# Bits of the keys as signs on ScalarE, the first head taken apart by VectorE alone, an expert picked by integer bits

## The chip, the cores and the metric

The kernel runs on one core of a Trainium2 chip. Its engines run side by side and wait for each other by semaphores: TensorE (PE in the rows; PEld is its weight load), VectorE (DVE), ScalarE (ACT), GpSimd (POOL) and SyncE (SP), which issues most transfers. The metric is the device time of one execution in microseconds, the median of several runs.

## The reference

Two layers follow each other. The first is attention in which a query sees only the keys of its own bucket; a bucket is the signs of six projections.

```python
q_bits = (np.einsum('bhsd,dk->bhsk', q, proj) > 0).astype(np.int64)   # k_bits likewise
q_bucket = np.sum(q_bits * powers, axis=-1)
mask = q_bucket[:, :, :, None] == k_bucket[:, :, None, :]
scores = np.where(mask, scale * np.matmul(q, k.transpose(0, 1, 3, 2)), -1000000000.0)
attn = np.exp(scores - np.max(scores, axis=-1, keepdims=True))
attn = attn / (np.sum(attn, axis=-1, keepdims=True) + 1e-09)
return np.matmul(attn, v)
```

There are 4 batches, 8 heads, 768 positions and 64 numbers per head. The result, 3072 tokens of 512 numbers, goes through a mixture of 8 experts: each token to the one expert with the largest logit, `h = relu(x @ w1[e])`, `y = h @ w2[e]`, weighted by the expert's probability.

## The kernel before

**Attention.** Two heads make a group, and there are 16 groups. A score tile is 128 queries by 768 keys; a group has 12 of them, all together 192 units. A step `c` of the main loop makes two scores, so there are 96 steps, and the steps overlap: in step `c` TensorE multiplies the weights of step `c-5` by the values (`pv`, L346), transposes the exponentials of step `c-2` in three batches of four (`trans`, L314) and makes two scores (`score`, L278 and L280). VectorE takes each score's row maximum (L285) and makes its factors (L286, L287), ScalarE the exponential (L295). A score tile has two places in PSUM, so score `i` waits for exponential `i-2`. Three places (`t`) serve the transposes, the projections of a group and the token rows.

**Taking apart.** Each 32-bit input is split in a rounded part and a rest, and both multiply. `qk` (later `w`) of a head has four planes of 768 columns: plane 0 is q rounded over q's rest, plane 1 is k rounded, plane 2 and plane 3 hold 80 rows: 16 rows of bits and the rest of the parts. `score` multiplies planes 0 and 1 (L280) and planes 2 and 3 (L278). The bits are scaled by a large number M0, so that a pair of different buckets falls far below every other score.

**Bits.** For a later group, `lsh_mm` (L232) projects both heads, `lsh_ev` (L243) copies the projections from PSUM, `lsh_bits` turns them into bits by two GpSimd operations (q's half at L237, k's half at L239, through the helper `bits`), and a store and a gather put them in the planes. For the two heads of the first group `lsh_first` (L217) projects, and `bits_first` makes the bits by VectorE straight from PSUM: for halves 0 and 1 of q at L237, for the halves 2 and 3 of k at L239. `split_first` takes these two heads apart with VectorE, ScalarE and GpSimd.

**The opening.** The order on every engine is the order in which the code is written. After the constants come `lsh_first(0)`, `split_first(0, 0)`, bits, `lsh_first(1)`, `split_first(1, 0)`, one bit operation, and then the loop with unit 0. The first three units are of head 0, the next three of head 1. In between `warmth` issues matmuls of ones (L99) that nothing reads.

**The pick.** Near the end of attention VectorE works out which expert has most tokens so far, in three steps of a generator (`pick_first`): keys (`keys`, L454 to L457), their maximum (L464, L466), and the expert's number (L468 to L471); SyncE loads it and starts to fetch that expert's weights. The loop takes the steps at `c` = NC-13, NC-11 and NC-10, where NC is 96. In the same stretch `tok_ev` (L375) scales token rows out of a `t` place.

Of the kernel before, what the change touches and what calls it, by code (L numbers as in the profile page):

```python
# [7 lines left out]
F32 = mybir.dt.float32  # L8
# [4 lines left out]
OP = mybir.AluOpType  # L13
# [17 lines left out]
M0 = float(2 ** 35)  # L31
# [10 lines left out]
WARM = 10  # L42
# [8 lines left out]
def lsh_attention_moe(ctx, tc, qk, qk2, v, proj, wg, w1, w2, out):  # L51
# [35 lines left out]
    load_x(1)  # L87
    ones = const.tile([128, 128], BF16, name="ones")
# [27 lines left out]
    lt6, lt12, eq12, thr, mul = (const.tile([128, 1], F32, name=n) for n in ("lt6", "lt12", "eq12", "thr", "mul"))  # L116
# [3 lines left out]
    nc.vector.tensor_scalar(thr, lt6, -LOW, LOW, op0=OP.mult, op1=OP.add)  # L120
    nc.vector.tensor_scalar(lt6, lt6, 1.5 * M0, None, op0=OP.mult)
# [64 lines left out]
    def split_first(h, half):  # L186

        x = XD[h]
        c = slice(half * HALF, (half + 1) * HALF)
        if half == 0:  # L190
            t = qk_tile(h)
            for a in range(2):
                nc.scalar.activation(t[:, 1, a * HALF:(a + 1) * HALF], x[:, S + a * HALF:S + (a + 1) * HALF], AF.Copy)
        t = QK[h]

        def copy(o, i):
            if half:
                nc.gpsimd.tensor_copy(o, i)
            elif h:
                nc.scalar.activation(o, i, AF.Copy)  # L200
            else:
                nc.vector.tensor_copy(o, i)

        copy(t[:, 0, c], x[:, c])
        copy(t[0:80, 2, c], x[0:80, c])
        (nc.gpsimd if h or half else nc.vector).tensor_tensor(t[64:128, 0, c], x[64:128, c], t[64:128, 0, c],
                                                              op=OP.subtract)
        if half == 0:
            for a in range(2):
                nc.gpsimd.tensor_tensor(  # L210
                    t[0:80, 3, a * HALF:(a + 1) * HALF], x[0:80, S + a * HALF:S + (a + 1) * HALF],
                    t[0:80, 1, a * HALF:(a + 1) * HALF], op=OP.subtract)
# [7 lines left out]

    def bits_first(h, a):
        bits(QK[h][0:16, 2 + a // 2, (a % 2) * HALF:(a % 2 + 1) * HALF], LP[-h][32 * a:32 * a + 16, :HALF],
             a < 2, thr[0:16], mul[0:16])
# [11 lines left out]
    def bits(o, i, q, th, mu, eng=nc.vector):  # L235
        if q:
# [532 lines left out]
    for c in range(NC + 2):  # L769
# [28 lines left out]
        if c and c <= NC:  # L798
            expo(2 * c - 2)
        if lsh:  # L800
            lsh_ev(g + 1)
# [215 lines left out]
```

## Time and profile before

| what | us |
|---|---|
| median of 3 runs (lowest, highest) | 794.73 (794.68, 794.74) |
| the profiled execution | 794.61 |
| its span | 792.8 |
| PE busy | 779.3 (98%) |
| POOL busy | 508.9 (64%) |
| DVE busy | 467.6 (59%) |
| ACT busy | 443.8 (56%) |

The profile is of one execution. Busy time of an engine is the time in which it has an instruction under way; the ends of matmuls are modelled, so a wait of TensorE that is shorter than such a tail does not show as idle time, but as a longer distance of one matmul to the next. PEclk is the share of full speed that the clock throttle granted; whether a matmul ran at the full or at the half level shows in the distances as well.

### The profile page before, as it was taken

The numbers are of one execution on the slowest core, as the hardware profiler recorded it, in microseconds if no ns is written. First come the engines' busy times: TensorE is split into PE (matmuls) and PEld (weight loads), VectorE is DVE, ScalarE is ACT, GpSimd is POOL, SyncE is SP. The second block draws the span as 40 slices with busy tenths as digits, with TensorE's granted clock in tenths as the row PEclk, the third lists the DMA queues.
The fourth block names the chain that finished last, engine by engine and source line by source line (L and its number), as shares of the span: only waits on it lengthen the run. The fifth ranks groups of instructions, "written<-read, shape, count | busy, mean of one in ns | idle before, by whom it ended". The sixth has DMA issues, their size and how long they took to land.

```text
span 792.8 us, 13715 instructions
## 1 busy us (share of the span) xinstructions
PE 779.3 (98%) x4829; PEld 617.1 (78%) x4829; DVE 467.6 (59%) x1092; ACT 443.8 (56%) x877; POOL 508.9 (64%) x620
## 2 busy tenths in 40 slices
PE   8999999999999999999999999999999999999995
PEld 4677677776677777777777768989999999989894
DVE  7777777877777777777787855232363632232221
ACT  4776676776767766677676741443434344434310
POOL 7877475686747678746769473585566666668431
PEclk9999999999999999999999999999999999999999
DMA  8389953265234236313336214844445455545201
GB/s 300 121 223 274 297 165 102 75 190 165 101 100 160 94 112 205 100 62 119 110 109 182 80 54 142 279 161 156 159 151 162 145 148 178 165 146 195 85 10 36
DMA packets 48071, 115.31 MB, mean 145 GB/s; under 512 B 8820, under 2 KB 12660, under 8 KB 48001
## 3 DMA queue, kind: packets, MB, share of 16 engines
q1 hardware_dynamic: 41184, 98.05, 38.9%
q0 software_dynamic: 6672, 16.35, 6.7%
q8 instruction: 39, 0.64, 0.3%
q14 instruction: 32, 0.25, 0.1%
q10 hardware_dynamic: 144, 0.02, 0.0%
HBM read 88.39 MB, written 26.51 MB: 145 GB/s over the span
## 4 chain that ended last, share of the span: by engine, by line
PE 89%; DVE 4%; issue 4%; POOL 1%; ACT 1%; DMA 1%; POOLq 0%; DVEq 0%; ACTq 0%
PE o L346 17%; PE t L314 16%; PE t L675 15%; PE t L701 9%; PE s L278 8%; PE s L280 8%; PE s L718 7%; PE t L365 4%; DVE m L285 2%; PE t L232 1%; PE s L727 1%; PE t L651 1%; PE s L675 1%; PE o L651 1%; POOL w L617 1%
## 5 line engine op out<-in xcount | busy, mean ns | idle before, releaser
L295 ACT ACTIVATE e<-s,m 128x768 f32<-128x768 f32 x192 | 190.4, 992 | 126.2 <-DVE m L287 123.8
L285 DVE TENSOR_REDUCE m<-s 128x1 f32<-128x768 f32 x192 | 182.9, 953 | 67.0 <-PE s L280 58.0
L617 POOL TENSOR_TENSOR w<-raw,w 128x512 fp32r<-128x512 f32 x112 | 142.4, 1295 | 44.5 <-ACT w L616 43.0
L314 PEld LDWEIGHTS t<-ident,e 128*128 128x128 f32 x1152 | 125.5, 140 | 42.5 <-issue 19.8
L314 PE MATMUL t<-ident,e 128*128 128x128 f32 x1152 | 147.3, 277 | 1.0 <-ACT bits L243 0.8
L346 PE MATMUL o<-pt,vt 128*64 128x384 f32 x768 | 144.8, 499 | 0.0
L675 PE MATMUL t<-xh,w 128*128 128x456 f32 (+6 forms) x672 | 126.9, 346 | 0.0
L675 PEld LDWEIGHTS t<-xh,w 128*128 128x128 f32 x672 | 119.2, 188 | 3.0
L336 ACT ACTIVATE pt<-t 128x512 f32<-128x512 f32 (+1 forms) x194 | 104.1, 593 | 1.1 <-PE t L314 1.0
L346 PEld LDWEIGHTS o<-pt,vt 128*64 128x64 f32 x768 | 46.6, 136 | 58.1 <-issue 54.5
L680 DVE SCALAR_TENSOR_TENSOR hh<-t,hh 128x256 fp32r<-128x256 f32 (+7 forms) x64 | 35.5, 554 | 89.2 <-ACT hh L679 87.8
L701 PE MATMUL t<-hh,w 128*128 128x456 f32 (+3 forms) x384 | 78.6, 358 | 0.0
L679 ACT ACTIVATE hh<-t 128x256 fp32r<-128x256 f32 (+7 forms) x64 | 31.4, 491 | 78.0 <-PE t L675 76.7
L731 POOL DMA_INDIRECT out_dram<-y,ix x27 | 26.9, 995 | 73.4 <-DVE y L729 32.7
L334 DVE COPY pt<-t 128x512 f32<-128x512 f32 (+1 forms) x97 | 66.1, 683 | 12.4 <-PE t L314 12.2
L701 PEld LDWEIGHTS t<-hh,w 128*128 128x128 f32 x384 | 69.9, 188 | 2.3
L616 ACT ACTIVATE w<-raw 128x512 fp32r<-128x512 f32 x112 | 66.3, 623 | 0.0
L718 PE MATMUL s<-w,hh 128*128 128x512 f32 (+2 forms) x264 | 64.5, 398 | 0.0
L237 POOL TENSOR_SCALAR bits<-bits 64x384 f32<-64x384 f32 x15 | 22.6, 1509 | 54.6 <-ACT bits L243 54.6
L718 PEld LDWEIGHTS s<-w,hh 128*128 128x128 f32 (+2 forms) x264 | 47.8, 185 | 11.2
L278 PE MATMUL s<-qk 80*128 80x384 f32 x192 | 53.9, 361 | 1.8 <-ACT e L295 1.8
L278 PE MATMUL s<-w 80*128 80x384 f32 x192 | 53.5, 360 | 0.0
(207 smaller groups left out, 1069.8 us busy)
## 6 DMA issues: line engine op xcount, KB each, us to landing
raw<-in_w_dram SPq DMA_DIRECT2D x64, 512.0 KB, 3.7
xd<-in_qk_dram SPq DMA_DIRECT2D x18, 768.0 KB, 4.4
xhe<-in_qk_dram SPq DMA_DIRECT2D x15, 768.0 KB, 7.4
w<-in_qk_dram SPq DMA_DIRECT2D x14, 768.0 KB, 4.7
sorted_rows<-xr SPq DMA_DIRECT2D x8, 1156.0 KB, 15.5
xg<-sorted_rows SPq DMA_DIRECT2D x25, 289.0 KB, 4.5
vt<-in_v_dram SPq DMA_DIRECT2D x16, 384.0 KB, 3.5
masks<-bits SPq DMA_DIRECT2D x15, 192.0 KB, 1.9
```

The source lines that it names most:

```text
L278: nc.tensor.matmul(p[:, a, :HALF], k[0:80, 2, c], k[0:80, 3, n], start=i >= 4, stop=i < 4)
L285: nc.vector.tensor_reduce(m[:, 0:1], p[:, :, :HALF], axis=AX.XY, op=OP.max)
L295: nc.scalar.activation(e, p[:, :, :HALF], AF.Exp, bias=m[:, 2:3], scale=m[:, 1:2], accum_out=SM[g, hf][:, t, s:s + 1])
L314: nc.tensor.transpose(p[:, x * 128:(x + 1) * 128], e[w][:, kt // 3, (kt % 3) * 128:(kt % 3) * 128 + 128], ident)
L334: nc.vector.tensor_copy(o, x)
L336: nc.scalar.activation(o, x, AF.Copy)
L346: nc.tensor.matmul(p[s * 64:(s + 1) * 64, :HALF], VT[g][:, kt, s, :], PT[u][:, s, kt, :], start=(kt == 0), stop=(kt == NT - 1))
L616: nc.scalar.activation(w[:, 0, a], r, AF.Copy)
L617: nc.gpsimd.tensor_tensor(w[:, 1, a], r, w[:, 0, a], op=OP.subtract)
L675: nc.tensor.matmul(p[:, :c], w[:, a, d, fs], x[:, b, d, :c], start=(k == 0), stop=(k == 11))
L701: nc.tensor.matmul(p[:, :c], w[:, a, f % 4, ms], h[b][:, f, :c], start=(k == 0), stop=(k == 23))
L718: nc.tensor.matmul(p[:pw], HH[n][b][:, f, i:i + pw], w[:, a, f % 4], start=(k == 0), stop=(k == 23))
```

## The change

A sign replaces the comparison. ScalarE makes sign(2^100 x - 2^-40) of the projections in one operation, +1 or -1, with the constant `small` as its bias. For the later groups this takes the place of ScalarE's copy, and GpSimd then only weighs q's half by `wsg`, one operation for two. For the first two heads the bits of k come as signs from PSUM, and VectorE keeps q's, with its weights. VectorE alone takes head 0 apart, GpSimd alone the q part of head 1. Head 1's projection moves behind score 0. The warm-up matmuls are 12 instead of 10 ahead of the first projection, and the three ahead of score 0 on head 1's side go. The pick takes the expert from the low three bits of the largest key, and its first step moves from NC-13 to NC-12.

```diff
-M0 = float(2 ** 35)
+M0 = float(2 ** 34)
+BIG = float(2 ** 100)
+TINY = float(2 ** -40)
...
-WARM = 10
+WARM = 12
...
+    small = const.tile([128, 1], F32, name="small")
+    nc.gpsimd.memset(small, -TINY)
...
+    nc.vector.tensor_scalar(wsg, lt6, 0.5 * M0, None, op0=OP.mult)
+    nc.vector.scalar_tensor_tensor(wsg, eq12, -3.0 * M0, wsg, op0=OP.mult, op1=OP.add)
...
-        copy(t[:, 0, c], x[:, c])
-        copy(t[0:80, 2, c], x[0:80, c])
-        (nc.gpsimd if h or half else nc.vector).tensor_tensor(t[64:128, 0, c], x[64:128, c], t[64:128, 0, c],
-                                                              op=OP.subtract)
-        if half == 0:
-            for a in range(2):
-                nc.gpsimd.tensor_tensor(
-                    t[0:80, 3, a * HALF:(a + 1) * HALF], x[0:80, S + a * HALF:S + (a + 1) * HALF],
-                    t[0:80, 1, a * HALF:(a + 1) * HALF], op=OP.subtract)
+        t = qk_tile(h) if half == 0 else QK[h]
+
+        def low(eng):
+            eng.tensor_tensor(t[64:128, 0, c], x[64:128, c], t[64:128, 0, c], op=OP.subtract)
+
+        if half:
+            nc.gpsimd.tensor_copy(t[:, 0, c], x[:, c])
+            nc.gpsimd.tensor_copy(t[0:80, 2, c], x[0:80, c])
+            low(nc.gpsimd)
+            return
+        eng = nc.gpsimd if h else nc.vector
+        for a in range(2):
+            nc.scalar.activation(t[:, 1, a * HALF:(a + 1) * HALF], x[:, S + a * HALF:S + (a + 1) * HALF], AF.Copy)
+        nc.scalar.activation(t[0:80, 2, c], x[0:80, c], AF.Copy)
+        eng.tensor_copy(t[:, 0, c], x[:, c])
+        low(eng)
+        for a in range(2):
+            eng.tensor_tensor(t[0:80, 3, a * HALF:(a + 1) * HALF], x[0:80, S + a * HALF:S + (a + 1) * HALF],
+                              t[0:80, 1, a * HALF:(a + 1) * HALF], op=OP.subtract)
...
+    def signs(o, i, at=0):
+
+        nc.scalar.activation(o, i, AF.Sign, bias=small[at:at + o.shape[0]], scale=BIG)
+
     def bits_first(h, a):
-        bits(QK[h][0:16, 2 + a // 2, (a % 2) * HALF:(a % 2 + 1) * HALF], LP[-h][32 * a:32 * a + 16, :HALF],
-             a < 2, thr[0:16], mul[0:16])
+        o = QK[h][0:16, 2 + a // 2, (a % 2) * HALF:(a % 2 + 1) * HALF]
+        i = LP[-h][32 * a:32 * a + 16, :HALF]
+        if a < 2:
+            nc.vector.tensor_scalar(o, i, thr[0:16], mul[0:16], op0=OP.is_gt, op1=OP.mult)
+        else:
+            signs(o, i, 32 * a)
...
-        nc.scalar.activation(BT[g], LP.pop(g)[:, :HALF], AF.Copy)
+        signs(BT[g], LP.pop(g)[:, :HALF])
...
-        bits(r[0:64], r[0:64], True, None, None, nc.gpsimd)
-        bits(r[64:128], r[64:128], False, thr[64:128], mul[64:128], nc.gpsimd)
+        nc.gpsimd.tensor_scalar(r[0:64], r[0:64], wsg[0:64], None, op0=OP.mult)
         nc.sync.dma_start(md[g], r)
...
-        nc.vector.tensor_tensor(k, first, C["desc"], op=OP.mult)
-        nc.vector.tensor_reduce(t[:, 1:2], k, axis=AX.X, op=OP.add)
+
         o = const.tile([128, 1], I32, name="o0")
-        nc.vector.tensor_scalar(o, t[:, 1:2], -1.0, float(E), op0=OP.mult, op1=OP.add)
+        nc.vector.tensor_scalar(o, t[:, 0:1], -1.0, None, op0=OP.add)
+        nc.vector.tensor_scalar(o, o, E - 1, None, op0=OP.bitwise_and)
+        nc.vector.tensor_scalar(o, o, -1.0, float(E - 1), op0=OP.mult, op1=OP.add)
...
-    lsh_first(1)
     split_first(1, 0)
-    bits_first(1, 0)
-    warmth(ps.tile([128, 512], F32, name="t", bufs=3), 3)
...
+        if c == 1:
+            bits_first(1, 3)
...
-        if c in (NC - 13, NC - 11, NC - 10):
+        if c in (NC - 12, NC - 11, NC - 10):
             next(pick)
...
+            if i == 0:
+                lsh_first(1)
+                bits_first(1, 2)
             if i == 1:
-                for a in (2, 3):
-                    bits_first(1, a)
+                bits_first(1, 0)
                 warmth(ps.tile([128, 512], F32, name="t", bufs=3), 9)
```

On ScalarE, from the taking apart of head 0 to the third exponential, stood before (`qk_142` is head 0, `qk_158` head 1, `xd` the loaded inputs, `s` a score, `e` its exponential; a row ends with the engines waited for):

```order
L193 ACTIVATE qk_142<-xd_70 128x384 [waits DMAHW1_49]
L193 ACTIVATE qk_142<-xd_70 128x384
L193 ACTIVATE qk_158<-xd_74 128x384 [waits DMAHW2_49]
L193 ACTIVATE qk_158<-xd_74 128x384
L200 ACTIVATE qk_158<-xd_74 128x384
L200 ACTIVATE qk_158<-xd_74 80x384
L295 ACTIVATE e_218,sm_186<-s_181,m_187 128x768 [waits DVE_49,PE_49]
L295 ACTIVATE e_220,sm_186<-s_194,m_199 128x768 [waits DVE_49,PE_49]
L295 ACTIVATE e_265,sm_186<-s_222,m_227 128x768 [waits DVE_49,PE_49]
```

There now stands (`qk_149` is head 0, `qk_160` head 1, `t_140` and `o_188` their projections in PSUM, L228 the signs):

```order
L212 ACTIVATE qk_149<-xd_70 80x384
L228 ACTIVATE qk_149<-t_140,small_76 16x384 [waits DVE_49,Pool_49]
L228 ACTIVATE qk_149<-t_140,small_76 16x384
L211 ACTIVATE qk_160<-xd_74 128x384 [waits DMAHW2_49]
L211 ACTIVATE qk_160<-xd_74 128x384
L212 ACTIVATE qk_160<-xd_74 80x384
L228 ACTIVATE qk_160<-o_188,small_76 16x384 [waits PE_49,Pool_49]
L301 ACTIVATE e_220,sm_183<-s_178,m_184 128x768 [waits DVE_49]
L228 ACTIVATE qk_160<-o_188,small_76 16x384 [waits DVE_49,Pool_49]
L301 ACTIVATE e_223,sm_183<-s_197,m_202 128x768 [waits PE_49]
L301 ACTIVATE e_268,sm_183<-s_225,m_230 128x768 [waits DVE_49,PE_49]
```

Two signs of head 0 have come in ahead of head 1's copies, one of head 1 ahead of the first exponential, and one, which waits for VectorE and GpSimd, between the first and the second.

On VectorE, from the subtraction of head 0 to the maximum of the third score, stood before (`o_153` is head 1's projection, L285 a row maximum):

```order
L206 TENSOR_TENSOR qk_142<-xd_70,qk_142 64x384 [waits DVE_49]
L237 TENSOR_SCALAR qk_142<-t_133 16x384 [waits DVE_49,PE_49]
L239 TENSOR_SCALAR qk_142<-t_133,thr_99,mul_100 16x384 [waits Pool_49] x2
L237 TENSOR_SCALAR qk_158<-o_153 16x384 [waits PE_49,Activation_49]
L285 TENSOR_REDUCE m_187<-s_181 128x1 [waits PE_49]
L286 TENSOR_SCALAR m_187<-m_187 128x1 [waits DVE_49]
L287 TENSOR_SCALAR m_187<-m_187 128x1 [waits DVE_49]
L285 TENSOR_REDUCE m_199<-s_194 128x1 [waits PE_49]
L286 TENSOR_SCALAR m_199<-m_199 128x1 [waits DVE_49]
L287 TENSOR_SCALAR m_199<-m_199 128x1 [waits DVE_49]
L239 TENSOR_SCALAR qk_158<-o_153,thr_99,mul_100 16x384 [waits Pool_49] x2
L285 TENSOR_REDUCE m_227<-s_222 128x1 [waits PE_49]
```

There now stands:

```order
L202 TENSOR_TENSOR qk_149<-xd_70,qk_149 64x384 [waits DVE_49]
L216 TENSOR_TENSOR qk_149<-xd_70,qk_149 80x384 [waits Activation_49] x2
L234 TENSOR_SCALAR qk_149<-t_140,thr_103,mul_104 16x384 [waits PE_49,Activation_49]
L291 TENSOR_REDUCE m_184<-s_178 128x1 [waits PE_49]
L292 TENSOR_SCALAR m_184<-m_184 128x1 [waits DVE_49]
L293 TENSOR_SCALAR m_184<-m_184 128x1 [waits DVE_49]
L291 TENSOR_REDUCE m_202<-s_197 128x1 [waits PE_49]
L292 TENSOR_SCALAR m_202<-m_202 128x1 [waits DVE_49]
L293 TENSOR_SCALAR m_202<-m_202 128x1 [waits DVE_49]
L234 TENSOR_SCALAR qk_160<-o_188,thr_103,mul_104 16x384 [waits Activation_49]
L291 TENSOR_REDUCE m_230<-s_225 128x1 [waits PE_49]
L292 TENSOR_SCALAR m_230<-m_230 128x1 [waits DVE_49]
```

The operations for the halves of k (L216) have come in, of six bit operations there two are left (L234), and the last of them stands behind the second score's factors and waits for ScalarE.

On VectorE around the first step of the pick stood before (`key0` are the keys, L427 ends a routing step, L285 is the next step's maximum):

```order
L427 RECIPROCAL xr_3538<-rf_4695 128x3 [waits DVE_49]
L454 TENSOR_TENSOR key0_4882<-base_122,base0_118 128x8
L456 COPY key0_c_4884<-key0_4882 128x8 [waits DVE_49]
L457 SCALAR_TENSOR_TENSOR key0_4882<-key0_4882,desc_114 128x8 [waits DVE_49]
L285 TENSOR_REDUCE m_4892<-s_4887 128x1 [waits PE_49]
L286 TENSOR_SCALAR m_4892<-m_4892 128x1 [waits DVE_49]
```

There now stands:

```order
L381 TENSOR_TENSOR xr_4905<-t_4901,r_4802 128x3x144 [waits DMASW6_49,DMASW7_49,DMASW0_49,PE_49]
L340 COPY pt_4844<-t_4907 128x2x2x128 [waits PE_49]
L460 TENSOR_TENSOR key0_4929<-base_129,base0_125 128x8
L462 COPY key0_c_4931<-key0_4929 128x8 [waits DVE_49]
L463 SCALAR_TENSOR_TENSOR key0_4929<-key0_4929,desc_121 128x8 [waits DVE_49]
L291 TENSOR_REDUCE m_4940<-s_4934 128x1 [waits PE_49,Activation_49]
```

The three operations of the keys have gone from behind the routing step to behind the scaling of the token rows (L381) and the copy (L340) of the step after.

## Rows read from the trace of the kernel before

**Rows 1.** Busy time by stretches: us, then each engine's, clock, DMA share, GB/s.

```profile
0.00:30.00 30.00, 25.11 (x141) 14.95 (x142) 24.22 (x62) 17.86 (x36) 24.91 (x39) 1.00 0.71 252
30.00:400.00 370.00, 370.00 (x2477) 262.79 (x2476) 280.85 (x669) 262.32 (x514) 252.83 (x334) 1.00 0.48 145
```

**Rows 2.** Chain of waits, 5 to 31 us: start, us, what.

```profile
13.26 0.68 DVE qk L239
...
26.80 0.62 PE s L278 x2
```

**Rows 3.** VectorE in order of time: start, us, line, operation, tiles, shapes, count.

```profile
5.28 0.62 DVE L202 CAST qk<-xd 128x384 fp32r<-128x384 f32 x2 [1.76 <-DMA xd<-in_qk_dram]
5.94 1.36 DVE L206 TENSOR_TENSOR qk<-xd,qk 64x384 fp32r<-64x384 f32 x1
...
7.91 1.38 DVE L239 TENSOR_SCALAR qk<-t,thr,mul 16x384 fp32r<-16x384 f32 x2
...
9.83 0.96 DVE L285 TENSOR_REDUCE m<-s 128x1 f32<-128x768 f32 x1
...
12.31 0.21 DVE L287 TENSOR_SCALAR m<-m 128x1 f32<-128x1 f32 x1
...
15.28 0.95 DVE L285 TENSOR_REDUCE m<-s 128x1 f32<-128x768 f32 x1
...
21.61 0.55 DVE L237 TENSOR_SCALAR qk<-o 16x384 fp32r<-16x384 f32 x1
```

**Rows 4.** GpSimd in order of time, the opening.

```profile
5.89 2.28 POOL L210 TENSOR_TENSOR qk<-xd,qk 80x384 fp32r<-80x384 f32 x2 [2.34 <-ACT qk L193]
```

**Rows 5.** VectorE's groups by line and shape: busy us, mean ns, idle before.

```profile
L657 DVE TENSOR_TENSOR xh<-o,xh 128x384 fp32r<-128x384 f32 x2 | 1.1, 558 | 5.7 <-ACT xh L656 5.7
```

**Rows 6.** ScalarE in order of time, the opening.

```profile
1.18 1.28 ACT L92 ACT_TABLE_LOAD   x1 [1.18 <-PEq L1010]
...
5.28 0.94 ACT L193 ACTIVATE qk<-xd 128x384 fp32r<-128x384 f32 x2 [2.60 <-DMA xd<-in_qk_dram]
...
12.62 0.99 ACT L295 ACTIVATE e<-s,m 128x768 f32<-128x768 f32 x1 [0.21 <-DVE m L287]
...
16.44 0.48 ACT L243 ACTIVATE bits<-t 128x384 f32<-128x384 f32 x1
```

**Rows 7.** TensorE in order of time, the opening and around 404 us.

```profile
1.07 3.85 PE L99 MATMUL o<-ones 128*128 128x512 bf16 x10 [1.07 <-DVE warm L91]
...
7.27 0.85 PE L217 MATMUL o<-xd,pj 64*32 64x384 f32 x8 [0.28 <-DMA xd<-in_qk_dram]
...
9.06 0.73 PE L278 MATMUL s<-qk 80*128 80x384 f32 x2
...
10.33 2.12 PE L99 MATMUL t<-ones 128*128 128x512 bf16 x9
...
13.84 0.59 PE L280 MATMUL s<-qk 128*128 128x384 f32 x2 [0.41 <-ACT e L295]
...
16.98 1.09 PE L314 MATMUL t<-ident,e 128*128 128x128 f32 x8 [0.82 <-ACT bits L243]
...
404.26 1.74 PE L314 MATMUL t<-ident,e 128*128 128x128 f32 x12
```

**Rows 8.** Chain of waits at 38, 67 and 405 us.

```profile
38.62 1.64 PE t L314 x12
...
67.13 1.46 PE t L314 x12
...
404.68 0.62 DVE xr L375
...
405.34 0.66 PE t L314 x4
```

**Rows 9.** VectorE in order of time, around 401 us.

```profile
400.96 0.95 DVE L456 COPY key_c<-key 128x8 f32<-128x8 f32 x1
...
406.81 0.96 DVE L285 TENSOR_REDUCE m<-s 128x1 f32<-128x768 f32 x1 [0.93 <-PE s L280]
```

## What the change does to the time, told before it was run

> **What bounds the kernel now.** I read the busy time by stretches first, then the chain of waits in the opening, and there the instructions of each engine in order of time. The table by stretches says where TensorE has room: from 30 to 400 us its matmuls fill 370.00 of 370.00, so nothing that shortens another engine's work there can shorten the kernel. In the first 30 us they fill only 25.11, warm-up matmuls included [rows 1]. The question is therefore when TensorE becomes continuously busy, and which small waits are left after that.
>
> In the chain the opening hardly belongs to TensorE. It runs over VectorE's bits (L237, L239), its row maxima (L285) and ScalarE's exponentials (L295), and reaches the matmuls for good only at 26.80 [rows 2]. So I replay the opening with the durations of before and carry the shift at 27 us through to the end.
>
> **The change part by part.**
>
> *Head 0 on VectorE.* Before, the 64-row subtraction took 1.36 us [rows 3], while GpSimd's two subtractions ran beside it, 2.28 for the pair [rows 4]. In the change GpSimd has no work between its constants and the landing of head 1 at 7.16. No row shows such a subtraction without a neighbour; the nearest is VectorE's two-input subtraction of 384 columns later on, 558 ns [rows 5]. Bounds: 0.36 (a cast of the width, from the pair's 0.62) and 1.36; I take 0.56, and 0.56 for each 80-row half too. Then: cast to 5.64, subtraction to 6.23, halves to 7.29 (instructions that wait for nothing overlap by 0.08; ScalarE's copies are there at 6.22 [rows 6]), the one bit operation left, 0.69 (half of L239's 1.38), to 7.99. Before, VectorE had all bits of head 0 at 9.29.
>
> *The signs.* A sign is a ScalarE operation on 384 PSUM columns with a bias pointer. The copy of that shape took 0.48 [rows 6], VectorE's operation with two pointers 0.69; these are the bounds, and I take 0.58 between them. The order shows that the first sign waits for VectorE; in the built program its count is that of VectorE's bit operation, not of the subtraction ahead of it. So it starts 0.1 after 7.99 (the hand-over from L287 at 12.52 to L295 at 12.62 [rows 3, 6]): 8.09 to 8.67, the second to 9.15. The masked half of score 0, whose matmuls ended at 9.79 [rows 7], ends at 9.65, and the first maximum starts at 9.69 for 9.83 [rows 3]. Of the 1.3 us that VectorE gained, the signs behind it take most.
>
> *Head 1.* ScalarE makes its copies only behind the signs (to 9.58 and 9.99, then q's to 10.41). GpSimd's first half waits for the first of them and ends at 10.67, the sign behind it at 11.35, and exponential 0 can start at 11.26. The bit matmuls of head 1 (0.78 us, the distance of L217's start from the next in its row's stretch) now stand between scores 0 and 1; score 1 is ready at 11.15, the second maximum starts at 11.19 and its factors end at 12.57, 0.05 later than before. Now comes the step that decides. VectorE makes the q bits of head 1, 12.61 to 13.28. The last sign of head 1 waits for VectorE, and the bits are the one thing that VectorE writes there; so 13.38 to 13.95. Exponential 1 stands behind that sign on ScalarE: it starts at 13.86, where it started at 12.62. Score 3 takes its place in PSUM and waits for it: 15.09 for 13.84 [rows 7], and its maximum starts at 16.06 for 15.28 [rows 3]. That is a loss of 0.78. That VectorE has one bit operation less there buys only 0.15, because the maximum of score 2 then waits for its matmuls: the nine warm-ups ahead of them (2.12 [rows 7]) now begin at 10.85 instead of 10.33.
>
> *To the end of the opening.* The two later q bits cost 0.69 for 0.55, 0.14 each at the most. The first ends 0.9 late; the transposes that wait for it started late before too, behind the evacuation at 16.92 [rows 6, 7], so 0.74 reaches the next maxima. The second, at 21.61 [rows 3], stands between maxima on the path: another 0.12. So 0.86 late when the values' matmuls start.
>
> *Fourteen later groups.* GpSimd loses one of two operations per group; TensorE has nothing to gain from it [rows 1], so 0. ScalarE's evacuation becomes 0.09 longer. In the stage at 38.6 the transposes waited for it, 1.64 us for twelve; in the next they did not, 1.46 [rows 8]. So +0.09 once; if every stage had to pay, 1.3; if none, 0.
>
> *The pick.* The key operations move one step on. Before, they delayed the maxima of their step (their copy alone 0.95 [rows 9]); the token rows were scaled late, and the third batch of transposes waited for that PSUM buffer [rows 8]: twelve took 1.74 where 0.11 each and the start make 1.5 [rows 7], of which I count 0.21. In the next step VectorE sat idle for 0.93 [rows 9], which covers most of what they take there: -0.21. The pick by bits is three small operations for three: 0. The two operations for the weights, the memset and two more warm-ups end before the first load lands at 5.28: 0.
>
> *Sum.* +0.86 + 0.09 - 0.21 = +0.74 on the profiled execution's 794.61 (792.8 of span and 1.8 around it) = 795.35; the median of the runs shown lies 0.12 above it, and with half of that the forecast is 795.4. Its own range, with the subtraction and the sign between most of their bounds: 794.9 to 796.0.
>
> A rule speaks against the signs. VectorE's operation on 384 PSUM columns takes 0.69, ScalarE's copy of them 0.48 [rows 3, 6]. The Trainium skill, "ScalarE: Activation LUTs", Rules for kernel authors, says to leave comparisons such as maxima, and multiplications, to VectorE, the faster one per element. By it a sign would be the dearer operation, and at 0.69 each the sum would be 795.6; by the rows it is the cheaper one, and what it costs is the hand-over.
>
> **The rivals.**
>
> A, the waits are not on the path: the signs start when their data are there, not when VectorE's bit operation has ended. Then the first starts at 7.39, the first maximum at 8.99, and through score 2 at 12.25 the maxima gain 0.7; less 0.24 for the dearer bits, plus the 0.12 that the last two terms gain together: 794.0. If only the last sign is freed, 794.6. For it: sign and bit operation only share a PSUM tile that both read. Against it: the order.
>
> B, the clock, on the slower side. The first ten warm-ups took 3.85 us, nine later ones 2.12 [rows 7]: most of the first ran at half pace, TensorE's lower level of 1.2 GHz. The change drops warm-ups, and between the first half of score 0, to about 7.3, and its masked half at 8.7 TensorE has nothing to do for 1.4 us. The longest such gap before was 1.0, ahead of the transposes at 16.98, and they ran at the full level behind it. If TensorE falls back in the longer one, score 1, the nine warm-ups and score 2 go at half pace: the warm-ups would end at 16.5, scores 2 and 3 come over 3 us late: about 798.5. It decides from the point where the nine warm-ups stand 0.43 apart.
>
> C, the subtraction stays at 1.36 without its neighbour, and the halves go to 1.0 (half of GpSimd's pair [rows 4], taken as the worst): 0.8 to 1.6 on top, 796.2 to 797.0.
>
> D, Sign needs another table. The one load took 1.28 [rows 6]; each of 14 groups would wait for two, some 33 us in all, about 835. The order shows a single load, as before. The Trainium skill, "ScalarE: Activation LUTs", Table sets: the hidden batching unit, warns that every switch between functions of different sets costs a load; no row here shows in which set Sign is.
>
> **How the numbers follow.** Forecast 0.65, A 0.16, B 0.09, C 0.06, D 0.01, small shifts of either sign 0.03. About 0.2%, 1.6 us, is what a measurement of this kernel can tell from no change: faster means under 793.1, slower over 796.3. A stays inside but for a tail of 0.03. Slower are B, D, most of C's half, and the forecast's tail with every evacuation exposed, 0.15 together; 0.82 is left for the same. The range goes down to A, 793.9, and up to C, 797.0; B, D and little else are left out.
>
> **What would show it.** Right: VectorE's first subtraction near 0.56, signs near 0.58, exponential 1 near 13.9 and right behind a sign, score 3 near 15.1, the values' matmuls near 28.5, and transposes without the wait near 405. Wrong: exponential 1 before 13 (A), the warm-ups behind score 1 at 0.43 apart (B), a subtraction over 1 us (C), more than one table load (D).

## The result

| kernel | median us (lowest to highest) | runs |
|---|---|---|
| before | 794.70 (794.54 to 794.85) | 6 |
| changed | 801.79 (800.85 to 801.85) | 6 |

The ratio is 1.0087, with a 95% interval of 1.0075 to 1.0099: the change costs 7.1 us. The forecast was 795.4 and its range ended at 797.0, so both were wrong, and on the slower side. The profiled execution of the changed kernel took 801.32, with a span of 799.5 against 792.8. In three of the runs below (the second operation of one column, and the last two) one execution each took 1102.19, 863.54 and 964.21 at a mean granted clock of 0.66, 0.85 and 0.75, and is not counted in the ratio.

First the busy time by stretches, in the changed kernel (columns as in [rows 1]):

```profile
0.00:30.00 30.00, 24.96 (x130) 14.32 (x132) 21.43 (x58) 19.25 (x38) 22.85 (x40) 1.00 0.71 252
30.00:400.00 370.00, 367.38 (x2438) 259.47 (x2436) 287.47 (x655) 259.67 (x505) 220.42 (x312) 1.00 0.46 144
```

TensorE, which filled 370.00 of 370.00 before, no longer does. GpSimd, the engine that was relieved, has 32 us less to do there. But VectorE has 6.6 us more, with fewer instructions in the stretch, though the change gives it no more work there. Something of VectorE's must last longer. Its groups by line and shape, in that stretch, first before and then changed (busy us, mean ns of one, idle before it):

```profile
L285 DVE TENSOR_REDUCE m<-s 128x1 f32<-128x768 f32 x156 | 148.6, 953 | 57.0 <-PE s L280 50.6 <-ACT ot L351 4.5 <-ACT pt L336 1.5
L355 DVE TENSOR_SCALAR r<-sm 128x6 f32<-128x6 f32 x26 | 4.6, 176 | 0.0
```

```profile
L291 DVE TENSOR_REDUCE m<-s 128x1 f32<-128x768 f32 x154 | 146.5, 951 | 46.6 <-PE s L286 40.3 <-ACT ot L357 3.9 <-ACT pt L342 1.9
L361 DVE TENSOR_SCALAR r<-sm 128x6 f32<-128x6 f32 x25 | 17.9, 717 | 0.0
```

The row maxima are as long as ever. What has grown is the smallest line of all: `sums` adds 1e-9 to six numbers per partition, once in three steps, and this addition (L355, now L361) takes 0.72 us on average instead of 0.18. Taken one by one over the whole kernel, eight of the 32 take 1.617 to 1.629, five 0.56 to 0.95, and nineteen 0.16. The mean hides that; the instructions of the line have to be read apart.

The place of the first one, with GpSimd beside it. Before (start, us, line, operation, tiles, shapes, count, idle before it):

```profile
39.86 0.32 DVE L355 TENSOR_SCALAR r<-sm 128x6 f32<-128x6 f32 x1
40.21 0.19 DVE L356 RECIPROCAL r<-r 128x6 f32<-128x6 f32 x1
```

```profile
39.65 1.50 POOL L237 TENSOR_SCALAR bits<-bits 64x384 f32<-64x384 f32 x1 [2.07 <-ACT bits L243]
41.25 1.66 POOL L239 TENSOR_SCALAR bits<-bits,thr,mul 64x384 f32<-64x384 f32 x1
42.98 0.83 POOL L177 CAST qk<-xd 128x768 fp32r<-128x768 f32 x1
```

And changed, VectorE, GpSimd, and then ScalarE and TensorE behind them:

```profile
41.29 1.62 DVE L361 TENSOR_SCALAR r<-sm 128x6 f32<-128x6 f32 x1
42.94 0.19 DVE L362 RECIPROCAL r<-r 128x6 f32<-128x6 f32 x1
43.05 0.93 DVE L291 TENSOR_REDUCE m<-s 128x1 f32<-128x768 f32 x1
```

```profile
40.85 1.24 POOL L255 TENSOR_SCALAR bits<-bits,wsg 64x384 f32<-64x384 f32 x1 [4.41 <-ACT bits L228]
42.06 0.81 POOL L186 CAST qk<-xd 128x768 fp32r<-128x768 f32 x1
```

```profile
44.53 0.99 ACT L301 ACTIVATE e<-s,m 128x768 f32<-128x768 f32 x1 [1.45 <-DVE m L293]
```

```profile
46.97 0.62 PE L284 MATMUL s<-w 80*128 80x384 f32 x2 [0.33 <-ACT e L301]
```

The addition starts 0.43 into GpSimd's multiplication and ends at 42.90, 0.03 after GpSimd's cast. The next row maximum waits for it, the exponential waits 1.45 for the maximum's factors, and the next score has no free place in PSUM until that exponential is done. Before, the second bit operation stood between the first and the cast, and by the time of the cast the addition was long over.

Why eight of fourteen groups? In all fourteen the addition starts inside GpSimd's multiplication, 0.43 behind its start in the eight and 0.48 in the six others. In the eight the next GpSimd instruction is the cast. In the six it is a copy of three whole numbers for the token rows, and there the addition takes 0.16 (VectorE, then GpSimd):

```profile
157.78 0.16 DVE L361 TENSOR_SCALAR r<-sm 128x6 f32<-128x6 f32 x1
```

```profile
157.30 1.24 POOL L255 TENSOR_SCALAR bits<-bits,wsg 64x384 f32<-64x384 f32 x1 [1.97 <-ACT bits L228]
158.50 0.18 POOL L440 COPY xr<-tokid_i 128x3 int32<-128x3 int32 x1
```

The starts of the values' matmuls, step by step (L346, now L352, from both traces), say what each place costs; between two rows nothing changes by more than 0.1:

| before | changed | later by | step | what is there |
|---|---|---|---|---|
| 27.70 | 29.12 | 1.42 | +1.42 | the opening |
| 41.62 | 42.85 | 1.24 | -0.19 | second group's projections |
| 45.92 ... 358.97 | 47.88 ... 365.83 | 6.86 | 8 x 0.68 to 0.72 | the eight long additions |
| 387.87 | 394.49 | 6.63 | -0.21 | an exponential that had started late |
| 407.35 | 413.72 | 6.37 | -0.23 | the pick, one step later |
| 430.56 | 437.27 | 6.71 | +0.33 | an addition of 0.56 beside GpSimd's subtraction |

That is 6.7 us, the whole difference of the spans. Each of the eight steps stands right behind one of the eight long additions. Of the five additions of 0.56 to 0.95, which stand beside GpSimd's subtractions, only the last shows as a step.

The opening, in the lines that the prediction spoke of. TensorE:

```profile
1.07 5.30 PE L104 MATMUL o<-ones 128*128 128x512 bf16 x12 [1.07 <-DVE warm L96]
6.30 1.08 PE L222 MATMUL t<-xd,pj 64*32 64x384 f32 x8
...
11.50 2.12 PE L104 MATMUL t<-ones 128*128 128x512 bf16 x9
...
15.58 0.58 PE L286 MATMUL s<-qk 128*128 128x384 f32 x2 [1.27 <-ACT e L301]
```

VectorE and ScalarE:

```profile
5.65 0.56 DVE L202 TENSOR_TENSOR qk<-xd,qk 64x384 fp32r<-64x384 f32 x1
6.23 1.02 DVE L216 TENSOR_TENSOR qk<-xd,qk 80x384 fp32r<-80x384 f32 x2
7.54 0.66 DVE L234 TENSOR_SCALAR qk<-t,thr,mul 16x384 fp32r<-16x384 f32 x1 [0.28 <-PE t L222]
...
16.57 0.96 DVE L291 TENSOR_REDUCE m<-s 128x1 f32<-128x768 f32 x1 [0.82 <-PE s L284]
```

```profile
8.30 1.17 ACT L228 ACTIVATE qk<-t,small 16x384 fp32r<-16x384 f32 x2 [1.70 <-DVE qk L234]
...
13.76 0.57 ACT L228 ACTIVATE qk<-o,small 16x384 fp32r<-16x384 f32 x1 [0.86 <-DVE qk L234]
14.36 0.99 ACT L301 ACTIVATE e<-s,m 128x768 f32<-128x768 f32 x1
```

They answer to [rows 3, 6, 7]: durations as forecast, the chain that was forecast over the sign of head 1, and all of it half a microsecond late. The twelve warm-ups are 0.43 apart to the last, so head 0's bit matmuls start at 6.30, a whole microsecond behind the data, and VectorE's bit operation waits for them.

### The profile page after: what moved, and what is told of

Its sections match the earlier page's. It is cut to its first block, busy times and chain, and to the rows that moved or that the text cites. A ratio compares the mean times of both kernels' runs of the same rounds, so it can differ in the third digit from the quotient of the medians.

```text
span 799.5 us, 13685 instructions
## 1 busy us (share of the span) xinstructions
PE 783.2 (98%) x4828; PEld 617.6 (77%) x4828; DVE 476.9 (60%) x1091; ACT 447.4 (56%) x881; POOL 476.7 (60%) x605
## 4 chain that ended last, share of the span: by engine, by line
PE 87%; DVE 5%; issue 4%; ACT 2%; POOL 1%; POOLq 0%; ACTq 0%; DVEq 0%
PE o L352 16%; PE t L320 15%; PE t L682 15%; PE t L708 9%; PE s L284 8%; PE s L286 7%; PE s L725 7%; PE t L371 4%; DVE m L291 2%; ACT e L301 2%; PE t L245 1%; PE s L734 1%; PE t L658 1%; PE s L682 1%; DVE r L361 1%
## 5 line engine op out<-in xcount | busy, mean ns | idle before, releaser
L352 PE MATMUL o<-pt,vt 128*64 128x384 f32 x768 | 144.8, 499 | 0.0
L352 PEld LDWEIGHTS o<-pt,vt 128*64 128x64 f32 x768 | 46.6, 136 | 58.1 <-issue 52.1
L340 DVE COPY pt<-t 128x512 f32<-128x512 f32 (+1 forms) x97 | 66.0, 681 | 12.4 <-PE t L320 12.2
L255 POOL TENSOR_SCALAR bits<-bits,wsg 64x384 f32<-64x384 f32 x15 | 18.6, 1243 | 63.0 <-ACT bits L228 63.0
```

What stands on the lines that cost most here:

```text
L340: nc.vector.tensor_copy(o, x)
L352: nc.tensor.matmul(p[s * 64:(s + 1) * 64, :HALF], VT[g][:, kt, s, :], PT[u][:, s, kt, :], start=(kt == 0), stop=(kt == NT - 1))
```

## The experiments

The theory from the trace: VectorE's addition is held while a GpSimd cast stands ready or runs, and taking one GpSimd operation out of each group moved the cast onto it. The rivals: the longer evacuation by Sign makes the stages longer; GpSimd ending earlier sets off something else; GpSimd's own load counts.

**The second GpSimd operation put back, as a multiplication by one.**

```
         nc.gpsimd.tensor_scalar(r[0:64], r[0:64], wsg[0:64], None, op0=OP.mult)
+        nc.gpsimd.tensor_scalar(r[64:128], r[64:128], one[64:128], None, op0=OP.mult)
```

Here `one` is a column of ones, made beside the other constants.

> The changed kernel with GpSimd's second operation per later group put back: it multiplies the 64 k rows by a column of ones, so the values stay as they are and GpSimd has more to do than in the changed kernel. Theory 1 (the cast): VectorE's small addition for the softmax sums (L361, 0.16 us) starts while GpSimd multiplies the q bits and stands still until the cast that follows them on GpSimd has ended, 1.62 us, in 8 of the groups; each of these makes TensorE 0.62 to 0.70 us later, 5.5 in all. With another multiplication between the first and the cast it isn't held, as before: 801.8 - 5.5 = 796.3 us, and no such addition over 0.4 us in the 8 groups. Theory 2 (the sign): ScalarE's sign, 0.58 for a copy of 0.49, is what makes the 8 stages longer: 801.8, and the stages stay 0.6 longer. Theory 3 (GpSimd's load): more work on GpSimd costs time: over 802.

Measured: 795.41, ratio to before 1.0005 (0.9995 to 1.0015). More work made the kernel 6.4 us faster (5.7 between the spans of the two profiles). The addition starts as far into the multiplication as in the changed kernel, and is not held:

```profile
41.14 0.16 DVE L364 TENSOR_SCALAR r<-sm 128x6 f32<-128x6 f32 x1
```

```profile
40.70 1.24 POOL L257 TENSOR_SCALAR bits<-bits,wsg 64x384 f32<-64x384 f32 x1 [3.62 <-ACT bits L230]
42.03 1.25 POOL L258 TENSOR_SCALAR bits<-bits,one 64x384 f32<-64x384 f32 x1
43.34 0.83 POOL L188 CAST qk<-xd 128x768 fp32r<-128x768 f32 x1
```

None of the eight steps is left in the stages (below 0.02 each); a new one of 0.43 at 412 us is met again with the three repairs. The sign is the same here, so the rival of the longer evacuation falls, and so does that of GpSimd's load. The multiplication alone does not hold the addition. What differs is the instruction behind it, and with the cast there the addition ended 0.03 behind that cast.

**The sums earlier in their step.**

```
             trans(c - 2)
+            if j >= 0 and j % 3 == 2:
+                sums(j // 3)
             trans_ev(1, True)
...
-        if j >= 0 and j % 3 == 2:
-            sums(j // 3)
```

> The changed kernel, with the softmax sums' two small VectorE operations (L361, L362) issued ahead of VectorE's evacuation of transposes in their step instead of behind it; GpSimd, ScalarE and TensorE have the same instructions in the same order. They then stand some 0.6 us earlier, ahead of GpSimd's multiplication. Theory 1 (the cast holds VectorE's addition): the additions take 0.16 in the 8 groups, and the 5.5 us come back: 796.3. Theory 2 (the sign is too long) and theory 4 (GpSimd ends earlier and something else, loads for instance, comes at a worse time): 801.8. If the two operations delay the evacuation behind them by 0.35, a little more than 796.3.

Measured: 796.25, ratio 1.0014 (1.0004 to 1.0025). Here GpSimd has the same instructions as in the changed kernel; only VectorE's two came forward, by 1.5 us in the first of the eight stages, where they now start a microsecond ahead of GpSimd's multiplication; and the eight steps are gone. So it isn't what an earlier GpSimd sets off elsewhere, it is who meets whom. At four other steps the stages lose 0.36, 0.23, 0.27 and 0.34, the last where the changed kernel loses 0.33. In the first and the third TensorE waits 0.25 and 0.20 for VectorE's evacuation of transposes (L340), which now stands behind the two operations; the other two show no such wait.

**Without the addition.** The sums go without their 1e-9.

```
-        nc.vector.tensor_scalar(r, SM.pop(divmod(u, 2)), 1e-9, None, op0=OP.add)
-        nc.vector.reciprocal(r, r)
+        nc.vector.reciprocal(r, SM.pop(divmod(u, 2)))
```

> The changed kernel without the small addition L361: the 1e-9 is left out of the softmax sums, and the reciprocal reads the sums itself and stands in the addition's place. All else is as in the changed kernel. Theory 1a (only an instruction of the addition's form is held by GpSimd): the reciprocal takes 0.19 everywhere, and the 5.5 us of the eight stages come back, 796.3. Theory 1b (any instruction of VectorE that reads and writes SBUF at this place is held): the reciprocal takes 1.6 in the eight stages, 801.8.

Measured: 795.20, ratio 1.0007 (0.9999 to 1.0016). The reciprocal has the addition's operand, stands at its place, and is never held, though the cast follows the multiplication as closely as in the changed kernel:

```profile
40.95 0.18 DVE L361 RECIPROCAL r<-sm 128x6 f32<-128x6 f32 x1
```

```profile
40.52 1.24 POOL L255 TENSOR_SCALAR bits<-bits,wsg 64x384 f32<-64x384 f32 x1 [4.42 <-ACT bits L228]
41.73 0.81 POOL L186 CAST qk<-xd 128x768 fp32r<-128x768 f32 x1
```

All 32 took 0.18. So the form of VectorE's instruction decides, not the place: theory 1a. The Trainium skill, "SBUF — State Buffer", Who interferes with whom, says that VectorE's copies, casts and tensor_scalar operations can take the pair of ports that it shares with GpSimd, that a reduction doesn't, and that the one that comes second is blocked for the whole of the other's instruction. The trace agrees on the forms (addition 1.62, reciprocal 0.18, row maxima unchanged). On who blocks whom it differs: the addition came 0.77 ahead of the cast and stood until that cast had ended.

**A second operation of one column.**

```
+        nc.gpsimd.tensor_scalar(r[64:128, 0:1], r[64:128, 0:1], one[64:128], None, op0=OP.mult)
```

> The changed kernel with a second GpSimd multiplication by one per later group, as in the run with the whole second operation, but of a single column instead of 384: it too waits for the multiplication of q's signs ahead of it, and costs GpSimd little. Theory 1 with the cast standing ready behind the multiplication as the cause: the cast is now kept back until the multiplication has ended, the additions take 0.16, and the 5.5 us come back: 795.4 to 796.3. If it is GpSimd's whole time in those steps that counts (the casts 1.3 later, as in the run with the whole operation): nothing comes back, 801.8, or part.

Measured: 795.69, ratio 1.0012 (1.0003 to 1.0021). The operation takes 0.30, the cast starts 0.46 behind the multiplication's end (1.40 with the whole operation, 0.03 ahead of it in the changed kernel), and all fourteen additions that fall into a multiplication take 0.16 to 0.17. So a short instruction that waits for the multiplication is enough when it stands between that and the cast; GpSimd's time doesn't count. Whether it has to wait is not shown: in the six other groups the copy behind the multiplication does not wait for it (it starts 0.04 ahead of its end), and those additions are not held either, but there no cast follows at once.

**The later groups' change alone, on the kernel before.**

```
-        nc.scalar.activation(BT[g], LP.pop(g)[:, :HALF], AF.Copy)
+        nc.scalar.activation(BT[g], LP.pop(g)[:, :HALF], AF.Sign, bias=small, scale=BIG)
...
-        bits(r[0:64], r[0:64], True, None, None, nc.gpsimd)
-        bits(r[64:128], r[64:128], False, thr[64:128], mul[64:128], nc.gpsimd)
+        nc.gpsimd.tensor_scalar(r[0:64], r[0:64], wsg[0:64], None, op0=OP.mult)
```

The constants that it needs come with it.

> The kernel before with the change of the later groups alone: signs by ScalarE instead of the copy, one multiplication of q's signs by GpSimd instead of two operations; opening, warm-ups and pick as before. Theory 1: the whole loss of the steady stretch is here, eight additions of 1.62 us: 794.7 + 5.5 = 800.2. If the additions are held only because the opening moved everything by 1.4 us: 794.7 to 795.5. Theory 2, every evacuation longer by 0.09 and paid: 796.0.

Measured: 805.17, ratio 1.0123 (1.0103 to 1.0144): slower than the whole change, and 5 us over what was expected. The eight steps are there, 0.67 to 0.70 each, with the opening at its old place; so the opening has no part in them. Two more of 0.3 stand at 202 and 316 us, and the rest comes at 421 us, where the old pick multiplies eight numbers by eight (VectorE, then GpSimd, then TensorE):

```profile
420.96 4.09 DVE L474 TENSOR_TENSOR key<-first,desc 128x8 f32<-128x8 f32 x1
```

```profile
420.54 0.96 POOL L443 DMA_INDIRECT sorted_rows<-xr,slot  x1 [0.23 <-issue]
421.50 0.84 POOL L184 CAST w<-xd 128x768 fp32r<-128x768 f32 x1
422.28 0.83 POOL L186 CAST w<-xd 128x768 fp32r<-128x768 f32 x1
423.06 1.95 POOL L188 TENSOR_TENSOR w<-xd,w 80x384 fp32r<-80x384 f32 x2
```

```profile
424.81 1.04 PE L320 MATMUL t<-ident,e 128*128 128x128 f32 x8
428.62 1.11 PE L320 MATMUL t<-ident,e 128*128 128x128 f32 x4 [2.78 <-DVE xr L381]
```

Before, it took 0.16. Now GpSimd reaches its casts while the multiplication stands there, and it is held for 4.09, until the last of five GpSimd instructions has ended at 425.01. TensorE waits 2.78 for the token rows; behind that gap four transposes take 1.11 (eight took 1.04 ahead of it), and the granted clock of 428 to 436 us is 0.57, between the full level of 2.4 GHz and half of it. This stage and the next lose 4.56 and 1.32. The new pick works on single numbers and stands elsewhere; the whole change escaped this by that.

**The last sign of head 1 behind exponential 1.**

```
-        if c == 1:
-            bits_first(1, 3)
...
             expo(2 * c - 1)
+        if c == 1:
+            bits_first(1, 3)
```

> The changed kernel with the last sign of head 1 issued behind exponential 1 on ScalarE instead of ahead of it; else the same. Theory 5 (the prediction's step on exponential 1): it starts near 13.1 instead of 14.36, score 3 near 14.4 instead of 15.58, its maximum near 15.75 instead of 16.57, so that some 0.8 us come back: 801.0. Rival: the maxima wait for something else by then (the transposes behind score 3, the sign of the next group) and nothing comes back: 801.8.

Measured: 800.60 (799.67 to 801.25), ratio 1.0065 (1.0049 to 1.0082). Exponential 1 started at 12.81, with no sign ahead of it. But the profile is of the execution that took 801.25, and in it the nine warm-ups, from 11.12 on, are 0.43 apart but for the first two and take 3.80 (granted clock of 11 to 14.4: 0.56), and score 2 comes at 14.36. That is the prediction's rival B, in a kernel near to the changed one. Three of the six runs lie at 799.7 to 800.0 and three at 801.2, on either side of the expected 801.0; whether the former kept the pace no profile shows. For the place of the sign the run with three repairs, below, tells more: its opening is 0.31 late, with ten warm-ups alone 0.98.

**Ten warm-ups at the start instead of twelve.**

```
-WARM = 12
+WARM = 10
```

> The changed kernel with 10 warm-ups at the start instead of 12; all else as in it. In its profile the twelve ran at half pace and kept TensorE until 6.3, where head 0's bit matmuls started; its first load had landed at 5.3. Theory 6 (the two more warm-ups are paid where the pace is low): head 0's bit matmuls start by 5.5, VectorE's bit operation ends near 7.9 instead of 8.20, and 0.3 to 0.9 us come back: 801.2. The prediction's step (they end before the load lands): 801.8.

Measured: 800.94 (800.84 to 801.09), ratio 1.0079 (1.0065 to 1.0093). Head 0's bit matmuls start at 5.45 instead of 6.30, and the values' matmuls of the first step 0.98 late instead of 1.42. Theory 6 holds: 0.44 in the stages of the two profiles, 0.85 by the medians. The medians say more than the profiles because four of the changed kernel's six runs took 801.74 to 801.85, half a microsecond over the profiled one.

**The pick's change alone, on the kernel before.**

```
-        if c in (NC - 13, NC - 11, NC - 10):
+        if c in (NC - 12, NC - 11, NC - 10):
```

with the three operations of the new pick in place of the old ones.

> The kernel before with the change of the pick alone (its keys one step later, the expert by integer bits). From the stages of the changed kernel, which come 0.21 and 0.23 nearer to those of before at 388 and 407 us: 794.65 - 0.44 = 794.2. Rival: by the prediction 0.21 of it, 794.45; or nothing.

Measured: 794.61, ratio 0.9998 (0.9989 to 1.0007). The expected 794.2 was missed; in the time nothing can be told. In the stages 0.22 is gained at 407 us, and nothing at 388; so that other 0.21 is not the pick's.

**Three repairs together.** The second operation, the sign behind exponential 1, and ten warm-ups, each as above.

> The changed kernel with three repairs together: the second GpSimd operation (multiplication by one) put back, the last sign of head 1 behind exponential 1, and 10 warm-ups instead of 12, so that head 0's bit matmuls start at 5.45 whatever pace the warm-ups have. From the run with the second operation alone, 795.4, less 0.8 to 1.2 for the sign's place: 794.3, 793.8 to 794.8. Rival: TensorE falls to its lower level in the opening, as in the profile of the run with the sign moved alone (its nine warm-ups 0.43 apart up to 14.3): 795.5 or more.

Measured: 794.89, ratio 1.0000 (0.9990 to 1.0010). The median is 0.1 above the range expected. The opening is 0.31 late instead of 1.42, the eight steps are gone; 0.41 is lost at 412 us, where the pick's keys, one step later now, stand beside GpSimd's two subtractions: their copy takes 0.88 and the operation behind it 0.93.

**Without the addition, the sign behind, ten warm-ups, and seven behind score 1.**

```
-                warmth(ps.tile([128, 512], F32, name="t", bufs=3), 9)
+                warmth(ps.tile([128, 512], F32, name="t", bufs=3), 7)
```

> The changed kernel with the small addition L361 left out (the 1e-9 on a sum of exponentials that holds exp(0) = 1 is below fp32's last bit, so the values stay), the last sign of head 1 behind exponential 1, 10 warm-ups at the start and 7 instead of 9 behind score 1. From the run with the three repairs, whose stages stood 0.31 late at 27.7 us and 0.09 late at the end: the hold at 412 us goes with the addition or stays (0.41 at most), and score 2 no longer waits for two of the nine warm-ups (up to 0.3): 794.1, 793.7 to 794.6. Rival: with fewer warm-ups TensorE falls to its lower level: over 795.5.

Measured: 794.16, ratio 0.9995 (0.9986 to 1.0005), the median as expected. But three of its runs took 795.49 to 795.73, about where the rival put it; the profile is of one at 794.16. In it the values start 0.09 earlier than before, and the last stages 0.6 earlier.

**And head 0's signs ahead of its bits of q.**

```
-    for a in (0, 2, 3):
+    for a in (2, 3, 0):
         bits_first(0, a)
```

> As the run before it, and head 0's two signs issued ahead of its bits of q: they then wait for VectorE's subtractions only, not for its bit operation, and the bit operation waits for them. Replay from the run with the three repairs: signs 6.97 to 7.54 and 7.56 to 8.14 instead of 8.02 to 9.19, the bit operation 8.24 to 8.90, so the masked half of score 0 can start 0.3 earlier, and the first maximum with it: 793.8. Rival: the first maximum then waits for something else (the first half of score 0, the warm-ups): same as the run before it.

Measured: 793.92, ratio 0.9994 (0.9984 to 1.0003); two of its runs took 795.38 and 795.49. The signs start at 6.91 instead of 7.97 in the run before it, the first maximum at 9.49 instead of 9.67, where 0.3 had been expected (and in this profile the first warm-ups were faster too), and the values' matmuls stand 0.26 ahead of the kernel before at 27 us and 0.80 at the end. The median is 0.8 below that of before; the interval still holds 1, so that it beats the kernel before is seen in the stages and not settled by the times.

## Why the prediction was wrong

**The step that failed** is the first sentence on the fourteen later groups: "GpSimd loses one of two operations per group; TensorE has nothing to gain from it [rows 1], so 0." A busy time of 370.00 in 370.00 says little of what can be gained (two stages in that stretch became 0.19 and 0.21 shorter, see below) and nothing of what can be lost. The step asked what TensorE could gain; it did not ask which instruction of GpSimd comes forward, and what runs on VectorE at that moment. At 40 us the cast started 3.12 behind the addition and now starts 0.77 behind it; eight additions became 1.46 longer, and 0.7 of each reached TensorE: +5.6. No rival had this mechanism, so no bound of the range could hold it.

**Two rows ahead of the prediction showed the effect.** The copy of eight keys at 400.96 took 0.95 [rows 9], and the prediction took this for what a copy costs. VectorE's other small operations there take 0.14 to 0.18, the same copy at 486.09 takes 0.17, and the GpSimd row beside it shows why this one doesn't:

```profile
400.87 1.01 POOL L184 TENSOR_TENSOR qk<-xd,qk 64x384 fp32r<-64x384 f32 x1
```

It ended at 401.88, and the copy at 401.91. And the subtraction of 1.36 beside GpSimd's 2.28 [rows 3, 4] was recognised as a neighbour's doing, since 0.56 was taken without it; but that thought stayed in the opening. Further on the same trace has a VectorE operation of a single column, 0.15 to 0.16 in five of its seven places, that starts 0.40 ahead of two GpSimd subtractions and lasts until the second has ended (VectorE, then GpSimd):

```profile
582.15 2.96 DVE L529 TENSOR_TENSOR spl<-spl 128x1 f32<-128x1 f32 x1
```

```profile
582.56 2.53 POOL L617 TENSOR_TENSOR w<-raw,w 128x512 fp32r<-128x512 f32 x2
```

**Point by point.** Head 0's subtraction is 0.56 and the two halves 1.02: right, and rival C fell with it. The signs take 0.57 and wait for VectorE, as the count in the program said: right, and rival A fell. There is one table load: D fell (its price does not add up: fourteen times two loads of 1.28 are 35.8, not 33, and would give 831, not 835). Exponential 1 stands behind the last sign and score 3 waits for it: right in order, and late by 0.5 at each point (14.36 for 13.86, 15.58 for 15.09, 16.57 for 16.06). This half microsecond is a wrong zero: "two more warm-ups end before the first load lands at 5.28" was reckoned from ten that took 3.85 [rows 7], of which the last ran at full pace. In the changed kernel the full pace came only after the twelfth. The run with ten shows its size, 0.44 in the stages. Without it the opening is +0.98 for a forecast +0.86.

The evacuation was forecast at +0.09 once, because the transposes at 38.6 had waited for it [rows 8]; no later stage pays for the sign, and the second group's is 0.19 shorter in every kernel with signs, with the old opening too. What had made the stage at 38.6 long was not the duration of ScalarE's copy. It started 0.44 behind the end of the projections, in the next three groups 0.11 to 0.12; in every kernel with signs it is 0.12 for this group as well (before, then changed):

```profile
39.06 0.49 ACT L243 ACTIVATE bits<-t 128x384 f32<-128x384 f32 x1 [0.66 <-issue]
```

```profile
40.17 0.58 ACT L228 ACTIVATE bits<-t,small 128x384 f32<-128x384 f32 x1 [0.35 <-issue]
```

The gain of 0.21 at 388 has the same look. The second exponential of that stage started 0.40 behind its factors (385.44), though its last wait had ended at 385.51, and now starts 0.12 behind them (392.28):

```profile
385.84 0.99 ACT L295 ACTIVATE e<-s,m 128x768 f32<-128x768 f32 x1 [0.50 <-PE t L314]
```

```profile
392.40 0.99 ACT L301 ACTIVATE e<-s,m 128x768 f32<-128x768 f32 x1 [0.22 <-PE t L320]
```

Both late starts are there in the run with the pick alone, which has ScalarE's instructions of before, and in no profile with signs, whether GpSimd has one or two operations per group. So GpSimd's relief did not give these 0.4 us; what had held the two instructions, the profile does not show. (Exponentials 0.33 late stand elsewhere in most of the profiles with signs, without a step.)

The pick's -0.21 was -0.23 in the changed kernel and -0.22 alone: right in size. The 0.95 that the prediction moved to the next step was no price, though: at its new place the copy takes 0.17.

Rival B did not show in the profile of the changed kernel (its nine warm-ups take 2.12), but did in that with the sign moved (3.80). The gap ahead of the masked half, from which the rival was argued, does not decide by itself: it is 1.14 in that profile and 1.52 in the last run's, whose warm-ups kept the pace. (The longest gap of before, 1.0 in the prediction, is 0.82 in its own row [rows 7].) The 0.09 given to B was not the reason for the miss.

**What stays open.** Why VectorE's addition, which starts ahead of the cast, is held through the rest of a multiplication that by itself holds nothing, is not shown by these traces. That it does not happen when another instruction than the cast stands next behind the multiplication is shown: a second multiplication that waits for the first, whole or of one column, and the copy of three numbers in six groups of the changed kernel. What held two ScalarE instructions of the kernel before, 0.33 each, is open too.

## What to carry to other kernels

When an engine is relieved, list what comes forward in its queue and what the other engines are doing at that time; between VectorE and GpSimd the small operations count as much as the large ones, for a 0.16 us addition in front of the row maxima cost 1.46. A tiny operation whose duration is many times that of its equals is a wait that the idle columns don't show: look at the neighbour's end before taking it as a price. And a busy share of 100% on one engine is no reason to put a change to another at 0.

## What the hardware showed

- GpSimd holds VectorE by form. Of VectorE's instructions with SBUF operands the additions (tensor_scalar, six columns), copies of four and eight columns and two-input operations of one, eight and 24 columns were held, the additions up to 1.64, the copies up to 1.27, the two-input operations up to 4.09. Not held in any of the thirteen profiles, though many fell into a GpSimd cast or two-input operation with 0.25 or more to go: reciprocals (103 such, none over 0.20), row maxima out of PSUM (931, none over 0.96), and tensor_scalar operations of a single column (the factors, L286 and L287, 2070, none over 0.22).
- Of GpSimd's instructions, casts and two-input operations held; its multiplications by a column alone did not (28 additions fell into one in the two runs with a second operation, all at 0.16 to 0.17). The 0.32 of the addition at 39.86 in the kernel before, in the first of fourteen such groups, isn't explained by this.
- The wait isn't limited to one instruction: the 4.09 lasted through the rest of an indirect store's issue, two casts and two subtractions.
- TensorE, after 2.78 us without matmuls, went on at half pace (granted clock 0.57 from 428 to 436 us): 4.56 were lost in that stage, wait and slow matmuls together, and 1.32 in the next.
- The pace of the first warm-ups differs between executions: ten took 3.85 to 4.45 in the profiles here, and twelve 4.48 to 5.30.
